# The transfers of the first weight blocks issued ahead of the first keys and queries

## Chip, cores and metric

One Trainium2 chip, one of its cores. The metric is the device time of one execution in microseconds (us), lower is better. The kernel before has a median of 1314.05 us in 3 runs (1313.09 to 1314.7).

## What is computed

Attention with a top-32 mask over 4 batches, 8 heads, 576 tokens, 64 numbers per head, then two gated layers on the 2304 resulting tokens of 512 numbers:

```python
scores = q @ k.T / sqrt(64)                        # 4 x 8 x 576 x 576
scores = where(scores >= 32nd largest of its row, scores, -1e9)
attn = softmax(scores); x = (attn @ v) as 2304 x 512
x = (sigmoid(x @ w_gate) * (x @ w_val)) @ w_out    # 512 -> 1536 -> 512
out = relu(x @ w_in)**2 @ w_out2                   # 512 -> 2048 -> 512
```

q, k and v are float32. The five weights arrive as float64, 34 MB in all.

## The kernel before

The tokens go in chunks: four of 128 (chunks 0 to 3), then seven of 256. Attention works in units, one unit being 128 rows of one head, and 8 units to a chunk of 128. For a unit TensorE makes the scores (`sp`, line 281), ScalarE copies them to SBUF (`S`, 284), VectorE takes the 32 largest of each row by four rounds of MAX8 and three of MATCH_REPLACE8 (`mx`, `W`, 294 and 300), GpSimd and ScalarE mask and exponentiate, TensorE transposes the weights (`tp`) and multiplies with v (`xp`). Keys and queries are first transposed on TensorE (`kpt` 158, `qpt` 244) and split in two parts (`kp`, `kl` 165 and 166; `qt` 256 and 257).

A weight is cut into blocks of 128 x 512, of 512 KB each: 12 of w_gate (`wg`), 12 of w_val (`wv`), 12 of w_out (`wo`), 16 of w_in (`wi`), 16 of the last weight (`w2`, whose tiles print as `w`). `conv` turns two blocks (a pair) to float32: per block ScalarE does two ACTIVATEs (466 and 447), VectorE one TENSOR_SCALAR for the pair (461) and one SCALAR_TENSOR_TENSOR per block (462), GpSimd one integer add per block (467). `scale` then needs products of the converted weight on TensorE (`wg_n`, 484), eight for each pair, and a maximum on VectorE (493). `split` makes two float16 parts of a pair (502 on ScalarE, 505 on VectorE or, for each fourth, 507 and 508 on GpSimd).

Chunk 0 goes through both layers in plain float32 with the converted weights (`moe32`, lines 750 to 833). From chunk 1 on the layers use the split weights in float16: `split_x` scales and splits a chunk's tokens (`x_1cm`, 545, is the maximum of chunk 1 on VectorE), the first layer follows (`pg`, `pv` 593; `acc` 633), its result is scaled in the same way (`x2pq` 666 on TensorE, `x2cm` 668 on VectorE, `x` 672 and 673), then the second layer (`ph` 696, `acc` 717).

Each engine runs its own list in order, SyncE (SP) the list of DMA issues. The order in these lists is made when the kernel is built: every instruction has a priority, which the schedule at the end of the program sets by `at(t)`, and attention heads are drawn forward by `high_priority` (`up[0]`); a planner then places instructions by priority and by its own view of what is ready. `fetch_to(i)` (406) issues the transfers of blocks up to number i, and of up to PREF = 4 blocks behind it while there are tiles left (WSLOTS = 35). Before the change it is called by `conv` alone, so that the first weight transfer has the priority of the first `weight_step`, which lies behind that of the first attention heads.

## Time and profile before

| | us |
|---|---|
| median of 3 runs | 1314.05 |
| profiled execution, span from the first to the last instruction | 1312.3 |
| TensorE busy (span share) | 1214.3 (93%) |
| VectorE busy | 1018.8 (78%) |
| GpSimd busy | 838.6 (64%) |
| ScalarE busy | 758.5 (58%) |

The profiled execution is given by its span alone; the median of the timed runs is 1.75 us above it. Busy shares are averages over stages with different limits, so the table by stage in the section of rows is to be read before them: an engine that is full in a stage sets how long the stage takes, and idle time of the others costs nothing there.

### The profile page before, as it was taken

Reading aid. Unit: us, or ns where it says so; the run is one execution under the profiler, and the core shown is the slowest. Engines: PE = TensorE matmul, PEld = TensorE weight load, DVE = VectorE, ACT = ScalarE, POOL = GpSimd, SP = SyncE. Lnnn points to the kernel's source line nnn. Section 1 sums busy time; section 2 is a strip of 40 time slices with the busy share of each in tenths; the row PEclk is TensorE's granted clock in tenths of the full one; section 3 lists DMA queues with packets and bytes.
Section 4 is the critical chain, followed back from the end, with each engine's and each line's share of the span. In section 5 each row is a group of like instructions: output and inputs, shape, how many; then the busy total and the mean of one; then the engine's idle time right before and its main releaser. Section 6 shows DMA issues by size and latency. Waiting matters only on the chain.

```text
span 1312.3 us, 28283 instructions
## 1 busy us (share of the span) xinstructions
PE 1214.3 (93%) x10613; PEld 971.6 (74%) x10613; DVE 1018.8 (78%) x2192; ACT 758.5 (58%) x1500; POOL 838.6 (64%) x1124
## 2 busy tenths in 40 slices
PE   6746798989999899999999999999999999999998
PEld 4535686777978778777888678777876887787775
DVE  6999999999999999989899888985998698210010
ACT  4876767677666665666566655664566566323122
POOL 1988878888676675586567746674576557324223
PEclk9766899999999999999999999999999999999999
DMA  6967861221323221524211233321111110000000
GB/s 187 350 246 252 276 206 56 62 64 54 94 67 103 61 62 28 132 70 137 82 53 36 73 101 96 95 67 53 42 48 42 46 37 10 17 2 1 17 1 16
DMA packets 116328, 113.00 MB, mean 86 GB/s; under 512 B 73440, under 2 KB 87776, under 8 KB 116192
## 3 DMA queue, kind: packets, MB, share of 16 engines
q1 hardware_dynamic: 116192, 111.19, 28.3%
q8 instruction: 84, 1.38, 0.4%
q14 instruction: 52, 0.43, 0.1%
HBM read 96.99 MB, written 14.16 MB: 85 GB/s over the span
## 4 chain that ended last, share of the span: by engine, by line
PE 70%; DVE 14%; POOL 6%; ACT 3%; DMA 3%; issue 3%; SPq 1%; ACTq 0%; POOLq 0%; DVEq 0%
PE acc L717 13%; PE ph L696 12%; PE pg L593 9%; PE pv L593 9%; PE acc L633 9%; PE xp L373 6%; PE sp L281 6%; PE tp L340 4%; DVE mx L294 3%; DVE W L300 3%; POOL W L307 1%; PE qpt L244 1%; DMA wv_r<-in_moe_w_val_dram 1%; DVE wv_c L462 1%; POOL W L322 1%
## 5 line engine op out<-in xcount | busy, mean ns | idle before, releaser
L294 DVE MAX8 mx<-W 128x8 f32<-128x576 f32 x432 | 327.4, 758 | 7.7
L307 POOL TENSOR_TENSOR W<-S,W 128x576 f32<-128x576 f32 x144 | 208.1, 1445 | 32.6 <-ACT W L306 32.1
L696 PE MATMUL ph<-x,wi_w 128*128 128x256 f16 (+1 forms) x1920 | 209.2, 260 | 8.0 <-ACT x L672 7.4
L300 DVE MATCH_REPLACE8 W<-mx,W 128x576 f32<-128x576 f32 x288 | 213.7, 742 | 0.0
L717 PE MATMUL acc<-w_w,rh 128*128 128x512 f16 x816 | 195.8, 379 | 1.5 <-POOL rh L709 1.5
L696 PEld LDWEIGHTS <-wi_w 128*128 128x128 f16 x1920 | 167.2, 99 | 39.7 <-issue 10.4
L306 ACT ACTIVATE W<-S,bs 128x576 f32<-128x576 f32 x144 | 112.0, 778 | 108.2 <-POOL bs L304 107.9
L593 PE MATMUL pg<-xs,wg_w 128*128 128x256 f16 (+1 forms) x1440 | 156.0, 257 | 3.1 <-ACT xs L547 1.6
L308 ACT ACTIVATE W<-W,bs 128x576 f32<-128x576 f32 x144 | 112.0, 778 | 71.8 <-POOL W L307 71.3
L593 PE MATMUL pv<-xs,wv_w 128*128 128x256 f16 (+1 forms) x1440 | 152.7, 257 | 0.2 <-DVE x2cm L668 0.2
L281 PE MATMUL sp<-kst,qt 128*128 128x288 f32 x608 | 130.6, 327 | 9.0 <-ACT S L284 5.0
L593 PEld LDWEIGHTS <-wg_w 128*128 128x128 f16 x1440 | 122.4, 98 | 18.3 <-issue 2.7
L633 PEld LDWEIGHTS <-wo_w 128*128 128x128 f16 x1440 | 123.1, 98 | 16.6 <-issue 3.7
L593 PEld LDWEIGHTS <-wv_w 128*128 128x128 f16 x1440 | 122.7, 98 | 16.4 <-issue 3.3
L717 PEld LDWEIGHTS <-rh 128*128 128x128 f16 x816 | 77.7, 98 | 76.4 <-POOL rh L709 2.0
L605 DVE TENSOR_TENSOR th<-pv,th 128x512 f32<-128x512 f32 (+1 forms) x60 | 36.2, 603 | 119.1 <-PE pv L593 117.9
L633 PE MATMUL acc<-gh,wo_w 128*128 128x256 f16 (+1 forms) x1200 | 124.8, 254 | 2.4 <-POOL gh L609 2.4
L294 DVE MAX8 mx<-S 128x8 f32<-128x576 f32 x144 | 107.4, 746 | 15.7 <-ACT S L284 15.4
L708 POOL TENSOR_TENSOR r<-r 128x512 f32<-128x512 f32 (+1 forms) x80 | 74.7, 936 | 59.8 <-ACT rh L707 58.8
L341 ACT COPY PT<-tp 128x512 f32<-128x512 f32 x144 | 83.7, 581 | 47.6 <-PE tp L340 39.3
L322 POOL TENSOR_SCALAR we<-W,rz 128x64 f32<-128x64 f32 x128 | 41.5, 324 | 108.0 <-DVE rz L313 72.7
L300 DVE MATCH_REPLACE8 W<-mx,S 128x576 f32<-128x576 f32 x144 | 106.8, 742 | 0.3 <-issue 0.3
(297 smaller groups left out, 2224.8 us busy)
## 6 DMA issues: line engine op xcount, KB each, us to landing
kst<-ks SPq DMA_DIRECT2D x104, 288.0 KB, 2.9
v<-in_v_dram SPq DMA_DIRECT2D x112, 128.0 KB, 2.2
qn<-in_q_dram SPq DMA_DIRECT2D x128, 64.0 KB, 2.2
wi_r<-in_moe_w_in_dram SPq DMA_DIRECT2D x16, 512.0 KB, 6.8
w_r<-in_moe_w_out_dram SPq DMA_DIRECT2D x16, 512.0 KB, 4.7
wg_r<-in_moe_w_gate_dram SPq DMA_DIRECT2D x12, 512.0 KB, 8.0
wv_r<-in_moe_w_val_dram SPq DMA_DIRECT2D x12, 512.0 KB, 7.2
wo_r<-in_moe_w_out_dram SPq DMA_DIRECT2D x12, 512.0 KB, 7.0
```

The source lines that it names most:

```text
L281: nc.tensor.matmul(sp[:, e, 0:HALF], l, r, start=(x == 0), stop=(x == len(ops) - 1))
L294: m8 = nc.vector.max(mx[:, r], cur)
L300: nc.vector.match_replace(wk, mx[:, r], cur, NEG)
L306: nc.scalar.activation(wk, ss, AF.Relu, bias=bs[:, 0:1], scale=-BIG)
L307: nc.gpsimd.tensor_tensor(wk, ss, wk, op=ALU.subtract)
L308: nc.scalar.activation(wk, wk, AF.Exp, bias=bs[:, 1:2], scale=SCALE, accum_out=bs[:, 2:3])
L341: nc.scalar.copy(ptr[:, :, i * P : (i + 1) * P], tp.rearrange("p (c t) -> p c t", c=CB))
L373: nc.tensor.matmul(xp[j * D : (j + 1) * D, o : o + n], vj, pj, start=(si == 0 and c == 0), stop=(c == NB - 1), skip_group_check=True,)
L593: nc.tensor.matmul(pp[:, e * N : (e + 1) * N], wblk(wd, a, c, f0, P), xs[:, b_, c, :], start=(e == 0 and n == 0), stop=(n == 3 * KM - 1), ...
L633: nc.tensor.matmul(acc[:, d // 2, (d % 2) * N : (d % 2 + 1) * N], wblk("wo", a, f, d * P, P), gh[:, b_, e * N : (e + 1) * N], start=(f == ...
L696: nc.tensor.matmul(ph[:, e * N : (e + 1) * N], wblk("wi", a, c, f0, P), x2[:, b_, c, :], start=(e == 0 and n == 0), stop=(n == 3 * KM - 1) ...
L717: nc.tensor.matmul(acc2[:, i, 0:DM], gh[:, b_, e * N + i * P : e * N + (i + 1) * P], wblk("w2", a, f, 0, DM), start=(f == 0 and x == 0), s ...
```

## The change

A constant FIRSTW = 4 is added. Ahead of the schedule's loop stands a new call of `fetch_to` for blocks 0 to 3, at a priority ahead of that of the first attention heads, and the condition in `fetch_to` no longer stops within the first FIRSTW blocks. Comments were taken out too, so line numbers differ by 1 to 6 behind the change.

```diff
+FIRSTW = 4
...
     def fetch_to(i):
         while fetched[0] < len(blocks):
             b = fetched[0]
             spare = b >= len(blocks) - M4RAW
-            if b > i and not (b <= i + PREF and (spare or live[0] + 3 <= WSLOTS)):
+            if b > i and (b >= FIRSTW or i >= FIRSTW) and not (
+                b <= i + PREF and (spare or live[0] + 3 <= WSLOTS)
+            ):
                 break
...
     tw, ta, tm = 0.0, CA0, None
     up[0] = AUP * 50
+
+    at(CA0 - 2 * AUP)
+    fetch_to(FIRSTW - 1)
     body = None
```

`fetch_to(3)` also takes the four blocks that PREF allows behind block 3, so it issues eight. The head of SP's list, before: `kn` and `ke` are keys, `qn` queries, `v` values, `ks` the split keys on their way to DRAM.

```order
L145 DMA kn_0_88<-in_k_dram 128x4x64 x2
L147 DMA ke_0_91<-in_k_dram 64x2x64
L215 DMA qn_0_111<-in_q_dram 128x2x64 x2
L224 DMA v_0_0_114<-in_v_dram 128x256
L227 DMA v_0_0_114<-in_v_dram 64x64
L224 DMA v_0_0_114<-in_v_dram 128x256
L227 DMA v_0_0_114<-in_v_dram 64x64
L172 DMA ks_0_106<-kp_0_93 64x576 x2
```

The same place in the changed kernel:

```order
L423 DMA wg_r_0_88<-in_moe_w_gate_dram 128x1024
L423 DMA wg_r_0_90<-in_moe_w_gate_dram 128x1024
L423 DMA wg_r_0_92<-in_moe_w_gate_dram 128x1024
L423 DMA wg_r_0_94<-in_moe_w_gate_dram 128x1024
L423 DMA wg_r_1_96<-in_moe_w_gate_dram 128x1024
L423 DMA wg_r_1_98<-in_moe_w_gate_dram 128x1024
L423 DMA wg_r_1_100<-in_moe_w_gate_dram 128x1024
L423 DMA wg_r_1_102<-in_moe_w_gate_dram 128x1024
L146 DMA kn_0_104<-in_k_dram 128x4x64 x2
L148 DMA ke_0_107<-in_k_dram 64x2x64
L216 DMA qn_0_127<-in_q_dram 128x2x64 x2
```

Eight weight transfers moved ahead of everything; before, the first of them stood in row 28 of the list. The planner follows them with the work on them. Head of VectorE's list before (keys, queries, then the first unit's maxima):

```order
L166 TENSOR_TENSOR kl_0_94<-kpt_0_0_95,kp_0_93 128x512
L166 TENSOR_TENSOR kl_0_94<-kpt_0_4_102,kp_0_93 128x64
L257 TENSOR_TENSOR qt_0_0_122<-qpt_0_119,qt_0_0_122 128x256
L294 MAX mx_0_185<-S_0_156 128x8
L300 MATCH_REPLACE W_0_184<-mx_0_185,S_0_156 128x576
```

In the changed kernel four pairs are converted first, and this is the end of them and what follows:

```order
L464 TENSOR_SCALAR wg_c_391<-wg_c_391 128x1024
L465 SCALAR_TENSOR_TENSOR wg_c_391<-wg_r_1_100,wg_c_391 128x512
L465 SCALAR_TENSOR_TENSOR wg_c_391<-wg_r_1_102,wg_c_391 128x512
L167 TENSOR_TENSOR kl_0_110<-kpt_0_0_111,kp_0_109 128x512
L167 TENSOR_TENSOR kl_0_110<-kpt_0_4_118,kp_0_109 128x64
L258 TENSOR_TENSOR qt_0_0_138<-qpt_0_135,qt_0_0_138 128x256
L464 TENSOR_SCALAR wg_c_405<-wg_c_405 128x1024
L465 SCALAR_TENSOR_TENSOR wg_c_405<-wg_r_2_314,wg_c_405 128x512
L465 SCALAR_TENSOR_TENSOR wg_c_405<-wg_r_2_316,wg_c_405 128x512
L295 MAX mx_0_201<-S_0_172 128x8
```

The first unit's first maximum moved from row 5 to row 20, behind the conversion of five pairs. On ScalarE's list four more ACTIVATEs 466 come between the steps of pair 2 and those 447 of pair 3; on TensorE's the `wg_n` products of pairs 1 and 2 stand ahead of the first `kpt`, those of pair 3 ahead of the first `qpt`, those of pair 4 among the first `sp`. The third place is VectorE's list where chunk 1's tokens are ready for the layers (`x_1cm`). Before, row 338 and those ahead of it:

```order
L313 RECIPROCAL rz_0_2348<-rz_0_2348 128x1
L505 SCALAR_TENSOR_TENSOR wo_w_1934<-wo_c_978,wos,wo_w_1934 128x1024
L300 MATCH_REPLACE W_1_2404<-mx_1_2405,W_1_2404 128x576
L294 MAX mx_1_2405<-W_1_2404 128x8
L294 MAX mx_2_2481<-S_2_2389 128x8
L300 MATCH_REPLACE W_2_2480<-mx_2_2481,S_2_2389 128x576
L294 MAX mx_2_2481<-W_2_2480 128x8
L545 TENSOR_REDUCE x_1cm<-x_1pq 128x1
```

In the changed kernel, row 349 and those ahead of it:

```order
L301 MATCH_REPLACE W_2_2480<-mx_2_2481,W_2_2480 128x576
L295 MAX mx_2_2481<-W_2_2480 128x8
L508 SCALAR_TENSOR_TENSOR w_w_2185<-w_c_1758,w2s,w_w_2185 128x1024
L301 MATCH_REPLACE W_2_2480<-mx_2_2481,W_2_2480 128x576
L295 MAX mx_2_2481<-W_2_2480 128x8
L508 SCALAR_TENSOR_TENSOR wi_w_2203<-wi_c_1381,wis,wi_w_2203 128x1024
L295 MAX mx_3_2561<-S_3_2444 128x8
L313 TENSOR_SCALAR rz_1_2419<-bs_1_2413 128x1
L548 TENSOR_REDUCE x_1cm<-x_1pq 128x1
```

Counted over the whole list, everything that stood ahead of `x_1cm` still does, and 11 rows more: five splits (two of w_in, two of w_out, one of the last weight), three MAX8, two MATCH_REPLACE8 and a small row. On TensorE's list 14 rows of chunk 0 (four `acc` 814, ten `ph` 797) that stood ahead of the products for `x_1cm` now stand behind them. From the maximum `x2cm` of chunk 2 (row 542 before, 544 after) the lists hold the same rows ahead of each place but for a few neighbours exchanged.

## Rows read from the trace of the kernel before

**Rows 1.** Table by stage: stretch in us, its length, then busy us (and instructions) of TensorE, its weight loads, VectorE, ScalarE, GpSimd, granted TensorE clock, DMA share, GB/s.

```profile
0.00:35.00 35.00, 23.30 (x81) 17.34 (x81) 23.65 (x50) 15.98 (x31) 7.14 (x18) 1.00 0.71 198
35.00:130.00 95.00, 58.08 (x370) 44.68 (x371) 94.78 (x156) 68.61 (x136) 85.32 (x65) 0.68 0.79 281
130.00:250.00 120.00, 99.35 (x806) 83.83 (x806) 114.36 (x208) 82.92 (x151) 100.58 (x91) 0.96 0.50 156
...
330.00:1120.00 790.00, 777.06 (x7017) 623.91 (x7015) 694.31 (x1590) 483.66 (x990) 514.59 (x797) 1.00 0.25 68
```

**Rows 2.** VectorE in order of time, at the maximum that opens chunk 1's layers and at the one that opens chunk 2's second layer; TensorE in order of time, at four products of chunk 0.

```profile
241.84 0.27 DVE L545 TENSOR_REDUCE x_1cm<-x_1pq 128x1 f32<-128x128 f32 x1
...
366.08 0.28 DVE L668 TENSOR_REDUCE x2cm<-x2pq 128x1 f32<-128x128 f32 x1
...
240.00 1.88 PE L814 MATMUL acc<-w_c,rr 128*128 128x512 f32 x4
```

**Rows 3.** Table by stage between these two maxima (columns as in Rows 1).

```profile
241.80:290.00 48.20, 43.27 (x576) 37.65 (x575) 46.65 (x94) 36.28 (x69) 40.39 (x51) 1.00 0.25 70
290.00:310.20 20.20, 16.20 (x174) 13.65 (x174) 19.90 (x42) 14.61 (x29) 16.43 (x19) 0.83 0.19 52
310.20:366.10 55.90, 53.52 (x705) 45.80 (x703) 52.74 (x122) 37.41 (x83) 42.91 (x75) 1.00 0.29 79
```

**Rows 4.** Waits of TensorE from 241.8 to 366.1 us: what waited for what, us in total, times, longest.

```profile
PE ph L696 <- ACT x L672: 3.3, 2, 2.7
PE acc L633 <- POOL gh L609: 1.7, 4, 0.6
PE pg L593 <- ACT xs L547: 1.6, 1, 1.6
PE acc L717 <- POOL rh L709: 1.5, 2, 0.8
PE tp L340 <- POOL W L322: 1.4, 4, 0.6
PE x2pq L666 <- ACT x L664: 0.9, 2, 0.5
PE pg L593 <- POOL xs L557: 0.7, 1, 0.7
```

**Rows 5.** VectorE in order of time (start and duration in us): where it idled in the first 30 us, with idle time and releaser in brackets.

```profile
6.47 0.82 DVE L166 TENSOR_TENSOR kl<-kpt,kp 128x512 fp32r<-128x512 f32 x2 [5.49 <-ACT kp L165]
8.35 0.42 DVE L257 TENSOR_TENSOR qt<-qpt,qt 128x256 fp32r<-128x256 f32 x1 [1.05 <-ACT qt L256]
11.36 0.76 DVE L294 MAX8 mx<-S 128x8 f32<-128x576 f32 x1 [2.59 <-ACT S L284]
...
28.80 0.15 DVE L312 TENSOR_SCALAR rz<-bs 128x1 f32<-128x1 f32 x1 [0.56 <-ACT W L308]
```

**Rows 6.** Transfers, from several views. In order: SP's issue of the first five weight blocks (start, us); ScalarE's wait for the first of them; issue to landing of all `wg_r` blocks; the same of the queries in the first 80 us; from the chain of waits the first keys and the last of the first 14 blocks (start, us); the stretch from 35 to 40 us (columns as in Rows 1).

```profile
25.57 2.51 SPq L420 DMA_DIRECT2D wg_r<-in_moe_w_gate_dram  x5
...
29.82 0.67 ACT L466 ACTIVATE wg_r<-wg_r 128x512 int32<-128x512 uint32 x1 [0.80 <-DMA wg_r<-in_moe_w_gate_dram]
...
DMA to landing us min/median/max: 4.2/8.0/9.7
...
DMA to landing us min/median/max: 1.8/2.3/7.3
...
1.46 3.13 DMA kn<-in_k_dram
...
36.03 9.52 DMA wv_r<-in_moe_w_val_dram
...
35.00:40.00 5.00, 4.21 (x26) 3.73 (x28) 5.00 (x10) 4.95 (x11) 4.21 (x3) 1.00 1.04 413
```

**Rows 7.** The instructions of one line or tile, durations in ns (min/median/max), then first and last start: a split and a conversion step on VectorE. Then ScalarE in order of time, at its pace of one conversion step after another.

```profile
L505 DVE SCALAR_TENSOR_TENSOR wi_w<-wi_c,wis,wi_w x7: 1261/1345/2040, 251.6 to 301.0; 128x1024 f16<-128x1024 f32 x7
...
L462 DVE SCALAR_TENSOR_TENSOR wg_c<-wg_r,wg_c x12: 668/678/1899, 33.1 to 58.5; 128x512 uint32<-128x512 uint32 x12
...
38.42 0.68 ACT L447 ACTIVATE wg_c<-wg_r 128x512 f32<-128x512 f32 x1
38.98 0.69 ACT L466 ACTIVATE wg_r<-wg_r 128x512 int32<-128x512 uint32 x1
```

**Rows 8.** Groups by form in the first 330 us (line, engine, operation, count, busy us, mean ns of one, idle before): conversion and splits on VectorE, conversion on GpSimd.

```profile
L462 DVE SCALAR_TENSOR_TENSOR wg_c<-wg_r,wg_c 128x512 uint32<-128x512 uint32 x12 | 11.3, 973 | 0.0
...
L505 DVE SCALAR_TENSOR_TENSOR wi_w<-wi_c,wis,wi_w 128x1024 f16<-128x1024 f32 x7 | 10.9, 1562 | 0.3 <-ACT wi_w L502 0.3
...
L505 DVE SCALAR_TENSOR_TENSOR wo_w<-wo_c,wos,wo_w 128x1024 f16<-128x1024 f32 x5 | 9.7, 1948 | 2.2 <-ACT wo_w L502 2.2
...
L505 DVE SCALAR_TENSOR_TENSOR w_w<-w_c,w2s,w_w 128x1024 f16<-128x1024 f32 x5 | 7.2, 1436 | 0.5 <-ACT w_w L502 0.5
...
L461 DVE TENSOR_SCALAR wg_c<-wg_c 128x1024 uint32<-128x1024 uint32 x6 | 5.9, 990 | 0.4 <-ACT wg_c L447 0.4
...
L467 POOL TENSOR_TENSOR wg_c<-wg_c,wg_r 128x512 int32<-128x512 int32 x12 | 19.1, 1620 | 1.3 <-ACT wg_c L447 0.7 <-DVE wg_c L462 0.6
```

**Rows 9.** VectorE in order of time: from one MATCH_REPLACE8 of a row block to its next, one MAX8 between.

```profile
25.05 0.74 DVE L300 MATCH_REPLACE8 W<-mx,S 128x576 f32<-128x576 f32 x1
...
26.70 0.74 DVE L300 MATCH_REPLACE8 W<-mx,W 128x576 f32<-128x576 f32 x1
```

## Prediction

> **What bounds the kernel now.** I read first the table by stage, because the busy shares of the whole span (TensorE 93%, VectorE 78%) hide that the limit changes. In the first 35 us no engine is full: VectorE works 23.65 us and idles 11.35. From 35 to 130 us VectorE is full (94.78 of 95), from 130 to 250 nearly so (114.36 of 120), while TensorE has gaps and runs partly at the lower of its two clock levels, 1.2 instead of 2.4 GHz (mean 0.68 of full speed from 35 to 130). From 330 to 1120 us TensorE is full, 777 of 790 [rows 1]. So the kernel has two parts: VectorE's, in which the weights are converted and split and chunks 0 and 1 get their attention, and TensorE's. The time is what TensorE's part takes, plus the time at which it can begin.
>
> Where it begins is read from two places. `x_1cm` at 241.84 us releases chunk 1's tokens for the layers; `x2cm` of chunk 2 stands at 366.08 [rows 2]. Between them TensorE is busy 43.27 + 16.20 + 53.52 = 113.0 of 124.3 us [rows 3]; of its 11.3 us of idle time, 6.5 are waits at the hand-over between layers (3.3 + 1.6 + 0.9 + 0.7) and 4.6 are waits for GpSimd (1.7 + 1.5 + 1.4) [rows 4]. The gaps that the change aims at are VectorE's at the start: 5.49 for the first keys, 1.05 for the queries, 2.59 for the first scores, 0.56 for a sum [rows 5].
>
> **The change part by part.** Nothing is added or removed but order: eight transfers of 512 KB stand ahead of the keys on SP's list, and the planner moves the conversion of these blocks, and more, ahead of attention on every engine.
>
> The keys' transfer. Before, the first keys land at 1.46 + 3.13 = 4.6 us. The first weight block of the run landed 4.2 us after its issue, and ScalarE did wait for it until 29.82. Fourteen blocks issued from 25.57 on had landed at 36.03 + 9.52 = 45.55, so the later ones came each (45.55 - 25.57 - 4.2)/13 = 1.21 us after the one before; 512 KB at the 413 GB/s of the stretch from 35 to 40 us is 1.27. Queries issued behind weights landed after up to 7.3 us, against a median of 2.3: a transfer waits for what was issued ahead of it [rows 6]. With the issues starting at 0.7 us, blocks land from 0.7 + 4.2 = 4.9 us on, 1.25 apart: 6.2, 7.4, 8.7, 9.9, 11.2, 12.4, 13.7. The keys follow at about 15, ten us later than before.
>
> VectorE's start. A pair needs both its blocks converted by ScalarE, 0.56 us a step [rows 7]. Pair 1 can begin on VectorE at 6.9 (6.2 and a step), pair 2 at 9.5. ScalarE's list then has four other steps ahead of pair 3's, the last of them on block 7 (12.4), so that pair begins at about 14.5, pair 4 at its heels. A pair takes VectorE 0.99 + 2 x 0.97 = 2.9 us in the mean, and 0.99 + 2 x 0.67 = 2.3 with its two block steps at their fastest [rows 7, 8]. Pair 1 ends at 9.2 with GpSimd idle, pair 2 at 12.4, pairs 3 and 4 at about 20. GpSimd adds at 1.62 us a block [rows 8], from 8.1 on, and TensorE's list has the products of pairs 1 and 2 ahead of the keys' transposes, those of pairs 3 and 4 ahead of the queries and among the scores. GpSimd is done with pair 2 at about 14.6, so the keys wait for nothing more than their landing; with pair 4 at about 22, which holds the first scores to about 24 and the first MAX8 to 24.6, against 11.36 before. VectorE has the keys, the queries and pair 5 to do in between. Its idle time by then: 6.7 (to 6.9), 0.3, 2.1, 1.0 (queries), 0.7, together 10.8 us. Before it was 11.35 [rows 1]. The hole at the start is filled with weights, but one of nearly the same size opens while weights land. Term: -0.5. Bounds: 6.7 if only the first wait stays (-4.7), and 10.8 plus 1.05 + 2.59 = 3.6, the waits for queries and scores of before [rows 5], if these start afresh when GpSimd is done (+3.1).
>
> Cheaper conversions. Pairs that meet an idle GpSimd cost 2.3 instead of 2.9. Of the four, the first is sure and the third likely: -1.2, between 0 and -2.4 (four times 0.6).
>
> Where chunk 1 comes in VectorE's list. Attention has been pushed behind weights, and the list shows how far it is still behind at `x_1cm`: five splits, three MAX8, two MATCH_REPLACE8 and a small row more stand ahead of it. A MAX8 and a MATCH_REPLACE8 take 1.65 us together [rows 9], so the attention rows take 2 x 1.65 + 0.75 + 0.1 = 4.1. The splits take 5 x 1.26 = 6.3 at their fastest [rows 7] and 2 x 1.56 + 2 x 1.95 + 1.44 = 8.5 at their means [rows 8]. That is 10.4 to 12.6; I take 11, nearer the low end, since rows overlap a little. VectorE is full here, so this is time on the path: `x_1cm` comes at 241.8 - 0.5 - 1.2 + 11 = 251.1.
>
> From there to the second place. The same TensorE work is left, plus 14 rows of chunk 0 that now stand behind chunk 1's first products instead of ahead of them: four 512-wide ones, 1.88 us [rows 2], and ten narrow ones at the stretch's mean, 113.0/1455 = 0.08 each, 0.8; together 2.7. So 115.7 us of work. VectorE is ahead with its splits, so I let the 4.6 us of waits for GpSimd go, and of the 6.5 at hand-overs I let the 14 rows fill the 2.3 at chunk 1's (1.6 + 0.7): 4.2 stay. 251.1 + 115.7 + 4.2 = 371.0, against 366.1: +4.9. With every wait kept (11.3) it is 378.1, +12.0; with none, 366.8, +0.7. VectorE isn't late here: it has 11 us less to do than before in a stretch that it filled for 119.3 us.
>
> Behind `x2cm` of chunk 2 both lists are the same but for neighbours, and TensorE is full [rows 1], so what is lost stays lost. I take +5: a span of 1312.3 + 5 = 1317.3 us. The timed median stands 1.75 above the profiled span, so **1319 us**. A measurement of this kernel can tell about 0.2% (2.6 us) from no change.
>
> **The rivals.** First, **filling the hole pays** (faster). VectorE's idle time is the first thing that one would cure. If the gaps while weights land are smaller than I think, near the 6.7 end, VectorE's part shortens by 4.7 + 1.2 = 5.9; if TensorE can then also catch up what chunk 1 comes later (VectorE has 11 us less to do behind `x_1cm`), the time is 1314 - 6 = 1308. For it: VectorE is full from 35 to 250. Against it: chunk 1's tokens do come later in the list, and TensorE has 113 us to do behind them. The Trainium skill, "Perfetto Trace Analysis", section "Optimization Strategy", says to find the gaps of the engine that limits a regime and make what it waits for start sooner; by that rule the change is right and this rival is the result. What the rows here add is that the gap filled must not be paid for in the start of the next regime.
>
> Second, **it comes out even**. VectorE's sum ahead of `x2cm` is the same set of rows; if TensorE's later start is covered by its 11.3 us of idle time entirely, only VectorE's own terms stay, -0.5 and -1.2, or the +0.7 of the case with no waits at all: 1312 to 1315.
>
> Third, **the keys' delay costs more** (slower still). Before, the chain from the keys over the transposes to the scores waited for nothing but itself; now it stands behind GpSimd's adds and the products of four pairs on TensorE. At its upper bound (+3.1) with no cheaper conversions `x_1cm` comes 14.1 late, and with the sum's own catching up behind it (11.3 of idle time less the 4.2 that stay, less 2.7 of added work: 4.4) 9.7 are left; with half of that catching up, 12: 1326. It decides from the place where GpSimd is later than 22 us with pair 4.
>
> Fourth, the change could do something other than it says: it does, since eight blocks go ahead, not four, but the list shows it, and the sum is made with eight.
>
> **How the numbers follow.** Chances: my forecast, chunk 1 later by some 9 us of which some 5 remain, 0.52; the keys' delay on top, 0.12; even, 0.20; filling pays, 0.16. The forecast's own range is 1315 to 1326 (+0.7 to +12.0). The range that should hold 8 in 10 must reach into the other cases: down to 1309, up to 1327. Slower by over 0.2%: 0.52 + 0.12, less 0.05 for the forecast's low edge, 0.59; within 0.2%: 0.20 + 0.05, of which 0.01 goes to faster, 0.24; faster: 0.17.
>
> **What would show it.** Right: the first `kn` landing near 15 us; VectorE's first MAX8 near 25; VectorE's idle time of the first 35 us near 11; `x_1cm` near 251 and `x2cm` of chunk 2 near 371, and from there on the same distance to the end. Filling pays, if VectorE's idle time is under 8 and `x2cm` comes before 364. The third rival, if the first MAX8 comes behind 28. I am wrong in the step from `x_1cm` on if that comes 10 us later and `x2cm` doesn't: then TensorE had more slack than its waits show.

## The result: 1.2% slower, three times the forecast

The changed kernel takes 1329.99 us, median of 4 runs (1328.17 to 1332.14), against 1314.38 of the kernel before in the same session (4 runs, 1313.09 to 1316.2): ratio 1.0119, 95% interval [1.0099, 1.0139]. That is +15.6 us; +5 was forecast, and the range ended at 1327. The profiled execution has a span of 1327.8 us, 15.5 more than before.

VectorE in order of time (start, duration, idle time in brackets), the first conversions, the queries and the first MAX8; they answer to [rows 5]:

```profile
6.70 0.69 DVE L464 TENSOR_SCALAR wg_c<-wg_c 128x1024 uint32<-128x1024 uint32 x1 [5.71 <-ACT wg_c L450]
7.43 1.29 DVE L465 SCALAR_TENSOR_TENSOR wg_c<-wg_r,wg_c 128x512 uint32<-128x512 uint32 x2
9.28 1.15 DVE L464 TENSOR_SCALAR wg_c<-wg_c 128x1024 uint32<-128x1024 uint32 x1 [0.56 <-ACT wg_c L450]
...
14.22 1.45 DVE L464 TENSOR_SCALAR wg_c<-wg_c 128x1024 uint32<-128x1024 uint32 x1 [1.51 <-ACT wg_c L450]
...
22.77 0.42 DVE L258 TENSOR_TENSOR qt<-qpt,qt 128x256 fp32r<-128x256 f32 x1 [1.05 <-ACT qt L257]
...
26.62 0.76 DVE L295 MAX8 mx<-S 128x8 f32<-128x576 f32 x1 [0.70 <-ACT S L285]
```

So far it is as forecast: pair 1 at 6.7 (6.9), pair 2 at 9.3 (9.5), pair 3 at 14.2 (14.5), the first MAX8 at 26.6 (24.6; 11.36 before). The table by stage (columns as in Rows 1), same stretches as there:

```profile
0.00:35.00 35.00, 14.68 (x76) 10.19 (x76) 23.77 (x32) 21.24 (x37) 20.52 (x20) 1.00 0.91 310
35.00:130.00 95.00, 48.79 (x250) 37.64 (x251) 94.59 (x159) 68.34 (x134) 77.18 (x65) 0.84 0.79 267
130.00:250.00 120.00, 98.85 (x807) 87.37 (x807) 112.84 (x209) 76.53 (x135) 84.69 (x82) 0.86 0.45 131
330.00:1120.00 790.00, 776.60 (x7060) 625.44 (x7057) 687.63 (x1573) 483.13 (x986) 510.30 (x796) 1.00 0.25 68
```

VectorE's column is that of [rows 1] to half a microsecond up to 130 us: one hole was filled, another opened. TensorE's is not: 76 + 250 instructions by 130 us instead of 81 + 370. Now the two places of [rows 2]:

```profile
255.51 0.29 DVE L548 TENSOR_REDUCE x_1cm<-x_1pq 128x1 f32<-128x128 f32 x1
...
310.98 0.29 DVE L671 TENSOR_REDUCE x2cm<-x2pq 128x1 f32<-128x128 f32 x1 [0.23 <-PE x2pq L669]
...
382.79 0.29 DVE L671 TENSOR_REDUCE x2cm<-x2pq 128x1 f32<-128x128 f32 x1 [4.63 <-PE x2pq L669]
```

The row in the middle is `x2cm` of chunk 1, which stood here before:

```profile
289.99 0.29 DVE L668 TENSOR_REDUCE x2cm<-x2pq 128x1 f32<-128x128 f32 x1 [0.30 <-PE x2pq L666]
```

`x_1cm` comes 13.7 us later, `x2cm` of chunk 1 21.0, that of chunk 2 16.7 later, and from there on the distance stays (16.3 at the last `x2cm`, 15.5 at the end). So 7.3 us more are lost in chunk 1's first layer, of which 4.3 come back by chunk 2's `x2cm`. There the whole loss exists. What the engines did until then is read from two stage tables (columns as in Rows 1), first of the kernel before, then of the changed one: up to `x_1cm`, from there to `x2cm`, and both.

```profile
0.00:241.80 241.80, 174.83 (x1206) 141.50 (x1207) 224.59 (x392) 161.09 (x305) 185.09 (x166) 0.85 0.66 216
241.80:366.10 124.30, 113.00 (x1453) 97.11 (x1452) 119.29 (x256) 88.30 (x180) 99.74 (x143) 0.97 0.26 72
0.00:366.10 366.10, 287.82 (x2657) 238.61 (x2658) 343.88 (x647) 249.39 (x484) 284.83 (x308) 0.89 0.52 167
```

```profile
0.00:255.50 255.50, 167.82 (x1171) 139.73 (x1172) 236.29 (x405) 170.29 (x313) 187.01 (x169) 0.87 0.64 204
255.50:382.80 127.30, 118.92 (x1488) 100.90 (x1487) 108.29 (x246) 82.21 (x175) 91.94 (x143) 0.99 0.25 70
0.00:382.80 382.80, 286.74 (x2657) 240.64 (x2658) 344.59 (x649) 252.50 (x487) 278.96 (x312) 0.91 0.51 160
```

The last row of each fence is the account. TensorE has done the same 2657 instructions in both, with 287.8 and 286.7 us of busy time; VectorE has worked 343.9 and 344.6. No work was added: the 16.7 us are idle time, on TensorE 96.1 instead of 78.3, on VectorE 38.2 instead of 22.2. VectorE's lie behind `x_1cm` (127.3 - 108.3 = 19.0 instead of 5.0), TensorE's ahead of it (87.7 instead of 67.0). Behind it TensorE idles a little less than before, 8.4 instead of 11.3, but has more to do. Its waits there answer to [rows 4]:

```profile
PE acc L636 <- POOL gh L612: 5.0, 5, 1.5
PE tp L341 <- POOL W L323: 1.2, 2, 0.9
PE xp L374 <- ACT PT L342: 0.9, 1, 0.9
PE ph L699 <- ACT x L675: 0.8, 1, 0.8
```

And this is the work of chunk 0 that TensorE still has behind `x_1cm` (groups by form: count, busy us, mean ns), before and, in the second fence, after:

```profile
L814 PE MATMUL acc<-w_c,rr 128*128 128x512 f32 x9 | 4.5, 610 | 0.0
L797 PE MATMUL ph<-x_plain,wi_c 128*128 128x128 f32 x12 | 1.5, 275 | 0.0
```

```profile
L817 PE MATMUL acc<-w_c,rr 128*128 128x512 f32 x20 | 9.3, 596 | 0.0
L800 PE MATMUL ph<-x_plain,wi_c 128*128 128x128 f32 x32 | 4.4, 275 | 0.0
```

13.7 us of chunk 0 stand behind `x_1cm` instead of 6.0.

### The profile page after: what moved, and what is told of

The parts are those of the page before. It is cut to its first block, busy times and chain, and to the rows that moved or that the text cites. A ratio compares the mean times of both kernels' runs of the same rounds, so it can differ in the third digit from the quotient of the medians.

```text
span 1327.8 us, 28308 instructions
## 1 busy us (share of the span) xinstructions
PE 1213.1 (91%) x10613; PEld 974.7 (73%) x10613; DVE 1021.1 (77%) x2192; ACT 762.8 (57%) x1500; POOL 829.7 (62%) x1124
## 4 chain that ended last, share of the span: by engine, by line
PE 75%; DVE 11%; POOL 4%; ACT 4%; DMA 3%; issue 2%; SPq 1%; ACTq 0%; POOLq 0%; DVEq 0%
PE acc L720 13%; PE ph L699 13%; PE acc L636 9%; PE pv L596 9%; PE pg L596 9%; PE xp L374 7%; PE sp L282 6%; PE tp L341 4%; DVE mx L295 3%; DVE W L301 2%; POOL W L308 1%; PE qpt L245 1%; DVE wi_c L465 1%; PE pg L753 1%; DMA w_r<-in_moe_w_out_dram 1%
## 5 line engine op out<-in xcount | busy, mean ns | idle before, releaser
L282 PE MATMUL sp<-kst,qt 128*128 128x288 f32 x608 | 133.3, 331 | 20.5 <-ACT S L285 12.7
L596 PEld LDWEIGHTS <-wv_w 128*128 128x128 f16 x1440 | 122.2, 98 | 15.2 <-issue 1.8
L282 PEld LDWEIGHTS sp<-kst,qt 128*128 128x128 f32 x608 | 91.3, 192 | 32.7 <-ACT S L285 14.4
```

The lines of the kernel that those rows point to most:

```text
L282: nc.tensor.matmul(sp[:, e, 0:HALF], l, r, start=(x == 0), stop=(x == len(ops) - 1))
L596: nc.tensor.matmul(pp[:, e * N : (e + 1) * N], wblk(wd, a, c, f0, P), xs[:, b_, c, :], start=(e == 0 and n == 0), stop=(n == 3 * KM - 1), ...
```

## The experiments

Each run has the kernel before beside it; differences below are against its median in the same session. This table holds what is compared. "Unit 8" is when VectorE ended the last MAX8 of chunk 0's attention, in brackets how many of the 34 pairs its list converts ahead of that; then the two places of above, and the number of instructions that TensorE had done by 241.8 us, read from stage tables.

| kernel | us against before | first MAX8 | unit 8 (pairs) | x_1cm | x2cm, chunk 2 | TensorE by 241.8 |
|---|---|---|---|---|---|---|
| before | 0 | 11.4 | 105.0 (16) | 241.8 | 366.1 | 1206 |
| changed | +15.6 | 26.6 | 130.9 (25) | 255.5 | 382.8 | 1058 |
| e1 four blocks | +18.0 | 17.7 | 137.2 (25) | 256.6 | 383.3 | 1040 |
| e2 behind the first unit | +15.9 | 11.3 | 113.6 (20) | 254.4 | 380.2 | 1109 |
| e3 splits held | +18.9 | 26.4 | 130.7 (25) | 252.6 | 384.5 | 1079 |
| e4 late keys alone | +22.3 | 27.6 | 127.7 (21) | 263.7 | 387.3 | 1003 |
| e5 early, held | +25.9 | 11.2 | 122.2 (16) | 260.3 | 392.0 | 1069 |
| e6 changed, held | +37.2 | 23.9 | 129.7 (16) | 267.3 | 397.9 | 1043 |
| e7 other order | +10.6 | 11.1 | 108.2 (17) | 245.6 | 377.7 | 1139 |
| e8 attention first, early | +34.8 | 11.2 | 110.0 (12) | 271.5 | 397.9 | 1062 |
| x1 emission only | +9.2 | 11.2 | 104.7 (16) | 241.0 | 376.1 | 1201 |
| x2 late layer | +9.9 | 11.0 | 104.7 (16) | 239.5 | 375.4 | 1174 |
| x3 attention first | +16.4 | 11.0 | 91.8 (12) | 253.9 | 381.7 | 1166 |
| x4 early, held whole | +18.3 | 11.1 | 113.8 (16) | 259.1 | 384.9 | 1111 |
| y1 spacing | 0.0 | 11.1 | 104.6 (16) | 236.8 | 366.4 | 1229 |
| y2 late shift | +1.5 | 11.2 | 104.6 (16) | 239.0 | 367.7 | 1222 |
| y3 early, near order | +19.3 | 11.3 | 116.9 (16) | 258.8 | 389.5 | 1134 |
| y4 behind two pairs of heads | +10.4 | 11.4 | 111.0 (18) | 246.7 | 378.6 | 1136 |
| z1 as y4, held | +14.8 | 11.2 | 116.3 (16) | 249.5 | 386.5 | 1148 |
| z2 four blocks, as z1 | +7.8 | 11.3 | 108.6 (16) | 243.9 | 372.0 | 1197 |

**e1, exactly four blocks.**

```diff
-    def fetch_to(i):
+    def fetch_to(i, pref=PREF):
...
-                b <= i + PREF and (spare or live[0] + 3 <= WSLOTS)
+                b <= i + pref and (spare or live[0] + 3 <= WSLOTS)
...
-    fetch_to(FIRSTW - 1)
+    fetch_to(FIRSTW - 1, 0)
```

> As the changed kernel, but exactly four blocks go ahead of the first keys (nothing behind them), so VectorE's list begins with the keys, the queries and the first MAX8 as before the change. VectorE's list at x_1cm is still that of the changed kernel: the same five splits, three MAX8 and two MATCH_REPLACE8 more stand ahead of it than before. Theory A, the place in the list (the loss is the rows that VectorE does ahead of x_1cm): x_1cm near 253, time near 1328. Theory B, the late start (the loss is what TensorE and VectorE don't get done while attention waits; 15.3 us at the first MAX8 have become 15.6 at the end, about one for one): the first MAX8 near 16.5, 5 us later than before, time near 1319.

1330.87 against 1312.85, ratio 1.0138 [1.0121, 1.0155]. The first MAX8 came 9 us earlier than in the changed kernel and nothing was won: theory B's 1319 is off by 12, theory A's 1328 by 3. Halving the blocks doesn't halve the loss.

**e2, eight blocks behind the first unit's keys.**

```diff
                 if n == 0:
-                    keys(0)
-                    pr.load()
-                    pr.load_keys(0)
-                    pr.queries(pr.tts[0:1])
+                    with tc.high_priority(offset=int(3 * AUP * 50)):
+                        keys(0)
+                        pr.load()
+                        pr.load_keys(0)
+                        pr.queries(pr.tts[0:1])
```

> All eight blocks ahead, but behind the keys, queries and values of the first unit, which are issued as before. VectorE's list at x_1cm (row 350) has the same five splits and five attention rows more ahead of it as in the changed kernel. Theory A: x_1cm near 253, time near 1328. Theory B: the first MAX8 at 11 to 12 as before, nothing lost at the start, 1312 to 1316; below 1312 if blocks that land some 15 us earlier then fill VectorE's first gaps.

1328.76, ratio 1.0122 [1.0107, 1.0137]. The first MAX8 stands where it stood before (11.26 us), and the loss is the whole +15.9. Theory B falls: it isn't the late first unit. Theory A's 1328 fits so far. But later units still come late: the second pair of heads' keys, now behind the blocks, land at 23.5 us instead of 12.7, and unit 3 ends at 51.1 instead of 30.7.

**e3, the extra splits held behind x_1cm.**

```diff
+    h0 = [t[1:] for t in todo].index(("wo", 3))
+    held, todo = todo[h0:], todo[:h0]
...
+    while 1 not in xsp:
+        attend(emitted[0] + 1, AHEAD)
+    p0 = tc.cur_priority
+    at(tm - SUP)
+    hold[0] = True
+    for t in held:
+        split(*t[1:])
+    tc.cur_priority = p0
```

(With `hold`, the ACTIVATE and the VectorE instruction of a split are ordered behind `x_1cm`.)

> As the changed kernel, but the splits from w_out's fourth on are held behind x_1cm by an order of the list without a wait on a semaphore: none of the five extra splits stands ahead of x_1cm. Theory A: x_1cm comes 5 x 1.4 = 7 us earlier, near 248.5, and the time falls to about 1323. Theory B: the splits were done in time that TensorE could not use anyway, x_1cm may come earlier but x2cm of chunk 2 stays near 383 and the time at 1328 to 1331.

1331.74, ratio 1.0144 [1.0128, 1.0159]. `x_1cm` comes 2.9 us earlier than in the changed kernel instead of 7, `x2cm` of chunk 2 1.7 later. Theory A falls too: the splits have to be done anyway, and the end doesn't care on which side of `x_1cm`.

**e4, late keys without early blocks** (the kernel before plus eight dummy transfers to DRAM).

```diff
     up[0] = AUP * 50
+    at(CA0 - 2 * AUP)
+    for kt in range(8):
+        t = dpool.tile([P, 1024], U32, tag=f"dm{kt}", name=f"dm_{kt}")
+        nc.sync.dma_start(t, w_out2[kt * P : (kt + 1) * P, 0:512].bitcast(U32))
```

> The kernel before, with eight transfers of 512 KB of the last weight into a scratch place in DRAM ahead of the first keys: the keys come late as in the changed kernel, but no weight block comes early and nothing is converted in the meantime; the output is the same. If the early conversions of the changed kernel are worth what they cost VectorE (four pairs at about 2.5 us, 10 us), this is about 10 us slower than the changed kernel, 1338 to 1342. Theory B (what counts is when attention begins, the early conversions return little): the first MAX8 near 22 to 26 and 1324 to 1331. Theory A: the same five splits stand ahead of x_1cm here, so 1328 plus the time that VectorE stands at the start, 1335 or more.

1335.10, ratio 1.0174 [1.0159, 1.0189]. With the keys late and no weight block early, 22.3 us are lost. That is 6.6 us above the changed kernel's +15.6. In the first 35 us VectorE works 10.66 instead of 23.77:

```profile
0.00:35.00 35.00, 9.48 (x39) 6.80 (x39) 10.66 (x19) 11.08 (x19) 7.12 (x11) 1.00 0.88 282
```

So the early conversions are worth something, some 7 us for 13 that VectorE worked more, but only where the change itself has made the hole. Theory A's "1335 or more" is met, but the planner exchanged rows here too (21 pairs ahead of unit 8 instead of 16), so not all of the 22.3 need be the keys'.

**e5 and e6, conversions held to their old place among the units.** NEED[p] is the number of units that stood ahead of pair p before the change; e5 has it on e2, e6 on the changed kernel.

```diff
+            maxima.append(m8.ins)
...
+                        i0 = nc.vector.tensor_scalar(ci, ci, 3, None, op0=ALU.logical_shift_left)
+                        if NEED[nstep[0]]:
+                            tc.add_manual_dep(
+                                i0.ins, maxima[min(NEED[nstep[0]], len(maxima)) - 1].name, NOSYNC, reason="behind a unit"
+                            )
...
-            elif tw <= ta and nstep[0] < len(steps):
+            elif tw <= ta and nstep[0] < len(steps) and emitted[0] >= NEED[nstep[0]]:
```

> Transfers as in the run with eight blocks behind the first unit's keys (1328.8), but each pair's conversion on VectorE is held behind the last MAX8 of the unit that it followed before the change: 16 pairs converted ahead of the last MAX8 of unit 8 (the end of chunk 0's attention) instead of 20, as before. Only VectorE's order is held, no wait is added. Theory C (early blocks are converted in place of attention; chunk 0's attention ends later, TensorE gets its layer-one products later and has the work to do when it is full): time 1311 to 1316, chunk 0's first product at 97 to 102. Theory D (the early transfers themselves cost, by what they take from keys and queries in the queue and on the DMA engines): 1326 or more, as without the hold.

> The changed kernel with the same hold: eight blocks ahead of the first keys, conversions behind the units that they followed before the change. Theory C: the loss from displaced attention goes, only the late start stays. Keys at 15 us instead of 4.6, VectorE stands still in between, the first MAX8 near 21: 8 to 10 us late, chunk 0's first product near 109, time 1322 to 1325. If the late start costs nothing by itself: 1312 to 1316. Theory D: 1330 or more.

1339.16, ratio 1.0196 [1.0174, 1.0219], and 1350.44, ratio 1.0282 [1.0252, 1.0312]. Both are far above what theory C allowed, and where theory D (the early transfers cost by themselves) put them. The waits of e5's TensorE in the first 60 us show one reason:

```profile
PE kpt L160 <- DMA kn<-in_k_dram: 16.4, 3, 9.7
```

It was 5.2 us in two waits before. The second pair of heads' keys are now behind the blocks, unit 3 ends at 35.9 instead of 30.7, and since the hold keeps conversions out of the hole, VectorE stands still. The second reason is in the last section. Theory C isn't tested cleanly by these two, but conversions kept out of attention's way didn't cure the loss.

**e7, another order without early blocks** (the kernel before).

```diff
-        head(0)
+        with tc.high_priority(offset=int(3 * AUP * 50)):
+            head(0)
```

> The kernel before with a higher priority for all that belongs to the start of attention (the second pair of heads' keys and queries too): no weight goes ahead of anything, but the planner's order shifts a little everywhere: 17 pairs instead of 16 ahead of unit 8's last MAX8, x_1cm at row 339 instead of 338. Theory C: one pair more is 3 us at chunk 0's first product, time 1314 to 1318. Theory E (the order before was a lucky one, and whatever shifts it costs some 15 us): near 1328.

1323.85, ratio 1.0080 [1.0058, 1.0102]: above theory C's 1314 to 1318, below theory E's 1328.

**e8 and x3, attention further ahead**: 12 pairs ahead of unit 8, in e8 on e5's transfers, in x3 on the kernel before, there held from ScalarE's two steps on (the diff shows the first).

```diff
-                nc.scalar.activation(c[:, e], r.bitcast(F32)[:, :, 1], AF.Copy, scale=REBIAS)
+                i0 = nc.scalar.activation(c[:, e], r.bitcast(F32)[:, :, 1], AF.Copy, scale=REBIAS)
+                if NEED[nstep[0]]:
+                    tc.add_manual_dep(i0.ins, maxima[min(NEED[nstep[0]], len(maxima)) - 1].name, NOSYNC, reason="behind a unit")
```

> Transfers as in e5, but held further: 12 pairs instead of 16 ahead of unit 8's last MAX8 (w_gate and w_val whole, which chunk 0's first layer needs), the others later. Theory C carried on: chunk 0's first product 8 to 12 us earlier, near 90, and as much of it as TensorE's wait for w_out's pairs doesn't take back: 1304 to 1311. If VectorE's total by x_1cm is the limit and not chunk 0's start: 1312 to 1320.

> The kernel before, with conversions held behind units from ScalarE's first step on (not only on VectorE as in e8): 12 pairs instead of 16 ahead of unit 8. Transfers as before the change. Theory C: unit 8 ends 8 to 10 us earlier, chunk 0's first product near 90, time 1306 to 1314. Theory F (conversions that are held meet GpSimd and cost VectorE 1.24 us a block step in place of 0.88, as in e5 and e8): unit 8 not before 105, time 1325 or more.

1348.04, ratio 1.0276 [1.0243, 1.0309], and 1329.64, ratio 1.0132 [1.0114, 1.0149]. x3 moves no transfer: unit 8 ends at 91.8, 13 us early, and the kernel is 16.4 us slower; chunk 0's first product stays at 99.2. Theory F fits in time only, since it wanted unit 8 behind 105. Attention further ahead doesn't pay either.

**x1 and x2, chunk 0's layers ordered behind a unit** (LATE = 8, where they stand anyway, and 10; no transfer or conversion is moved).

```diff
-            if body is None and ci in xsp:
+            if body is None and ci in xsp and emitted[0] >= LATE:
...
+                        if fp == 0 and t == e == c == 0:
+                            tc.add_manual_dep(mm.ins, maxima[LATE - 1].name, NOSYNC, reason="behind a later unit")
```

> The kernel before, with chunk 0's first product ordered behind the last MAX8 of unit 8, where it stands anyway: nothing moves on purpose, VectorE's list has the same pairs ahead of each unit (16 ahead of unit 8), TensorE's list the same row for the first product. The planner still exchanges neighbours. Theory C (what counts is when chunk 0's attention ends and its layers can begin): first product near 100, time 1313 to 1317. Theory E (any exchange costs some 10 us, the order before is a lucky one): 1322 to 1328, as with the other order (1323.9).

> As x1, but chunk 0's first product is ordered behind the last MAX8 of unit 10: no transfer and no conversion is moved, VectorE still has 16 pairs ahead of unit 8, only TensorE begins chunk 0's layers some 27 to 32 us later, as in the changed kernel (128.9 against 99.8). Theory C: TensorE's work that can't be done early has to be done when it is full: 1323 to 1330, and 8 us or more above x1. If TensorE makes up for it, because it waits for w_val and w_out in the kernel before anyway: within 3 us of x1.

1322.44, ratio 1.0070 [1.0052, 1.0088], and 1323.14, ratio 1.0075 [1.0058, 1.0091]. In x2 the first product starts at 141.3 us, later than in the changed kernel (129.0), and it costs 0.7 us over x1: theory C falls, the late start of chunk 0's layers is no price by itself. But x1, which should have done nothing, lost 9.2, as theory E had it. Its stage up to `x2cm` of chunk 2:

```profile
0.00:376.10 376.10, 297.46 (x2657) 247.47 (x2658) 342.49 (x649) 253.20 (x487) 288.22 (x312) 0.86 0.51 162
```

The same 2657 instructions, idle 78.6 us as before (78.3), but 297.5 us busy instead of 287.8: x1 loses its 10 us in how long TensorE's instructions take, at a mean granted clock of 0.86 of full speed instead of 0.89. The changed kernel loses idle time at 0.91. They are different losses.

The other runs can be read in the same way, since TensorE has done 2657 instructions at this place in each of them. Against the kernel before, e7, x1, x2 and x3, which have no transfers ahead, show 0.3 to 5.8 us more idle time and 5.8 to 11.6 more busy time. z2 and y4 show 5.4 and 6.5 more idle time, all other runs with transfers ahead, e4's dummies among them, 10.7 to 27.9. In one profiled execution of each, idle time of TensorE is the mark of the transfers, slower instructions that of a shifted order.

**x4 and y3, early blocks held from ScalarE's steps on** (e2's transfers; x4 holds both ACTIVATEs of a block, y3 the first).

> As e5 (eight blocks early behind the first unit's keys, 16 pairs ahead of unit 8), but held from ScalarE's steps on, so that ScalarE's second step of a block doesn't run ahead and GpSimd's adds come when they came before the change. Theory F: VectorE's block step falls from 1.24 to about 0.9 us, 20 us less in all; unit 8 ends near 108 to 112 (second pair of heads' keys still 5 us late), time 1314 to 1322. If the early transfers themselves are the cost: 1330 or more as in e5.

> Eight blocks early behind the first unit's keys, conversions held on ScalarE's first step so that the lists come as near to those of before as they get: 16 pairs ahead of unit 8, x_1cm at row 337, 100 products of chunk 1's second layer ahead of chunk 2's maximum, and x2cm of chunk 2 and 3 at the rows of before (542, 680). Theory H: second pair of heads' keys 5 us late, 1316 to 1321. Theory G: 1322 to 1332. If the early transfers are a cost by themselves, near 1331 to 1339 as in x4 and e5.

1331.49, ratio 1.0139 [1.0120, 1.0157], and 1333.30, ratio 1.0143 [1.0117, 1.0170]. VectorE's block steps cost 0.96 and 1.02 us in the mean instead of e5's 1.24, so theory F names a true part of e5 (x4 is 7.6 us below it), but not 20 us. The rest stays, with unit 3 again 7 us late (37.8 and 38.0). Both are in the ranges that their texts gave for early transfers as a cost by themselves (1330 or more, 1331 to 1339).

**y1 and y2, small shifts of the kernel before** (CA = 6.1 instead of 6.0; SWI = 4 instead of 5).

> The kernel before with one number of the schedule changed by 2% (the distance of attention's priorities, 6.0 to 6.1). Transfers, the start and VectorE's list are the same up to row 188; behind it neighbours are exchanged (x_1cm stays at row 338, 104 products of chunk 1's second layer ahead of chunk 2's maximum on TensorE's list instead of 109). Theory G (the order of before is one that the planner's rules rarely find; whatever shifts it costs 8 to 11 us from x_1cm to x2cm of chunk 2): 1320 to 1326. Theory H (what counts there is how much of chunk 1's second layer TensorE has ahead of chunk 2's maximum: 109 before, 8 after the change, 72, 48 and 34 in three controls): 1313 to 1316.

> The kernel before with the last conversions of w_in asked for one step of chunk 0's layers earlier: the lists are the same up to VectorE's row 252, and 113 products of chunk 1's second layer stand ahead of chunk 2's maximum. Theory G: 1319 to 1326. Theory H: 1312 to 1316.

1313.98, ratio 0.9997 [0.9986, 1.0009], and 1315.51, ratio 1.0007 [0.9993, 1.0021]. Theory G, that any shift costs, falls, and theory E with it.

**y4, z1 and z2, blocks behind two pairs of heads** (e7's edit on the changed kernel; z1 with y3's hold; z2 with e1's edit too).

> Eight blocks ahead, but behind the keys, queries and values of the first two pairs of heads (units 1 to 4): 18 pairs instead of 16 ahead of unit 8, x_1cm at row 339 as before, and 8 products of chunk 1's second layer ahead of chunk 2's maximum as in the changed kernel. Theory H: x_1cm near 245, time 1324 to 1330. Theory G: 1320 to 1328 too. If what costs is VectorE's list at the start (pairs ahead of unit 8: 16 before, 20 to 25 in the early kernels), about 2 pairs x 2.5 = 5 us: 1317 to 1320.

> Transfers as in y4 (eight blocks behind the keys, queries and values of the first two pairs of heads), but conversions held on ScalarE's first step, so that 16 pairs instead of 18 stand ahead of unit 8's last MAX8, and 92 products of chunk 1's second layer ahead of chunk 2's maximum instead of 8. Theory I (the blocks don't cost by themselves; they cost where VectorE converts them in place of attention, or where later heads' keys come late behind them): unit 8 ends near 106 as before, time 1314 to 1319, 5 us or more below y4 (1324.4). If the hold itself costs what it saves, as in x4 and y3 against e2: 1324 to 1332.

> As z1, but four blocks, exactly; the lists come nearest to those of before of all kernels with early blocks (16 pairs ahead of unit 8, x_1cm at row 338, x2cm at rows 413, 542 and 680 as before). Theory I: 1313 to 1317. If early blocks cost whatever their place: above 1322.

1324.38, ratio 1.0074 [1.0055, 1.0093]; 1331.15, ratio 1.0117 [1.0092, 1.0141]; 1324.12, ratio 1.0074 [1.0046, 1.0101]. Theory H fits y1, y2 and y4, but not y3, of which it wanted 1316 to 1321. y4 has the same edit as e7, on the changed kernel instead of the kernel before, so e7 is its control: +10.4 and +10.6 us, `x2cm` of chunk 2 at 378.6 and 377.7. y4's blocks are issued from 14.56 us on, e7's from 20.21. Behind the keys of two pairs of heads the earlier blocks cost nothing that shows beyond the shift of order.

Theory I fails as a forecast: with 16 pairs ahead of unit 8 z1 is slower than y4 with 18. Its units 1 to 3 end as before (30.7), unit 4 at 52.1 instead of 44.4: TensorE waits 5.9 us for the third pair of heads' keys, and VectorE converts three pairs between unit 4's first MAX8 and its next step. In time z1 and z2 are where their texts had them if the blocks or the hold cost anyway (1324 to 1332, above 1322). z2, with half the blocks, is level with y4 in ratio; these two are the best of the kernels with early blocks, and slower than before. No run beat the kernel before.

## Why the forecast was right in sign and wrong in size

**The start was right**, the keys (landed at 14.3 and 14.9 us, forecast 15), the order of the pairs, the first MAX8 to 2 us, the idle time: 35 - 23.77 = 11.2 us in the first 35 against 11.35, forecast 10.8. A hole of the same size opened while blocks land. (The transfer issued at 36.03 us is the thirteenth block, not the fourteenth, so the pace worked out from it is 1.32 us, not 1.21; the sum took 1.25, and the eight blocks landed 1.29 apart.)

**"Cheaper conversions" had the wrong sign.** -1.2 was taken; they cost 3.8 us more. The 68 block steps on VectorE went from 59.9 to 64.8 us, the 34 pair steps from 38.1 to 37.0. The first and the third pair were cheap, as forecast (1.29 us for two block steps each), the later ones dearer, most of all the last weight's and w_in's:

```profile
L465 DVE SCALAR_TENSOR_TENSOR w_c<-w_r,w_c 128x512 uint32<-128x512 uint32 x16 | 17.1, 1105 | 0.0
L465 DVE SCALAR_TENSOR_TENSOR wi_c<-wi_r,wi_c 128x512 uint32<-128x512 uint32 x16 | 16.6, 1075 | 0.0
```

(890 and 826 ns before.) The step priced the four pairs that are moved, not the thirty whose surroundings change with them. What changed there is how long the block steps wait for GpSimd (last section).

**"Where chunk 1 comes in VectorE's list" was right in its rows.** 11 was taken; the splits came to +4.0 us (26.4 instead of 22.4) and the attention rows to +4.3, 8.3 in all. With 3.8 for conversions, 2.0 more idle time, and what small rows and overlaps take off, that is the 13.7 at `x_1cm`, where 9.3 had been forecast.

**"From there to the second place" is the step that failed most.** It let TensorE catch up 4.4 us, to 115.7 of work and 4.2 of waits; measured are 118.9 and 8.4, 3.0 us more than before instead of 4.4 less. These 7.4 us, and 4.4 by which `x_1cm` came later than forecast (255.5 instead of 251.1), are the 11.8 between 371.0 and 382.8. Two terms are off. The 2.7 us of chunk 0's work behind `x_1cm`, counted from rows of the list, were 7.7: the list tells the order, not how far TensorE has got when VectorE reaches a row. (The rest of the work took 1.8 us less than before, at a granted clock of 0.99.) And the 4.6 of waits for GpSimd, let go because VectorE would be ahead with its splits, became 6.2 (5.0 + 1.2). "VectorE isn't late here" was true and no use: it idles 19.0 us there.

**What replaced it.** Attention came later, and with it TensorE's work. The second pair of heads' keys landed at 29.4 us instead of 12.7, and up to 130 us VectorE was as full as before, but on weights: 25 pairs ahead of unit 8 instead of 16. TensorE had done 447 instructions at 160 us instead of 599, and 1058 instead of 1206 at 241.8. Behind that TensorE is nearly full and gets little of it back. The last column of the table shows this across kernels: 1197 to 1229 go with losses of 0 to 9 us, 1109 to 1174 with 10 to 19, 1079 and fewer with 15.6 to 37. That is a regularity over 20 kernels; no run varied it alone. Among the rivals, "the keys' delay costs more" came nearest in time (1326). Its mark, a first MAX8 behind 28, wasn't reached, and e2 loses as much with the first unit on time. But its subject was the right one: late keys without early blocks lose 22.3 us in e4. It priced the first keys and left out the later ones, which stand behind the blocks in e2 too.

**The rule** of the Trainium skill, "Perfetto Trace Analysis", section "Optimization Strategy", says to make what the limiting engine waits for start sooner. Here its gain shows, some 7 us between e4 and the changed kernel, and is less than the 22.3 us that e4 loses without it.

**What stays open.** How the 15.6 us divide between the late keys, the conversions in attention's place, and the order that the planner happens to find. As far as e4 tells, late keys are enough for such a loss, and with conversions held to their old place it remains (e5, e6, x4, y3), so theory D, that the transfers cost by what they take from keys and queries, survives for blocks that stand ahead of the second pair of heads' keys: the nine such kernels, the changed one among them, lose 15.6 to 37. Behind those keys it isn't shown: y4 and z2 lose no more than the shift e7, z1 loses 14.8. And the shifts e7, x1 and x2 lose 9 to 11 where y1 and y2 lose next to nothing; why is open, but in x1 and x2 it is mostly busy time. A kernel with the early transfers and every other list untouched wasn't tried.

## What to carry to other kernels

When transfers move ahead, ask what then stands behind them, not only for the first keys but for the next ones, and what the scheduler will do with the data that come early. Here VectorE was as busy as before and TensorE starved, and TensorE pays later, when it is full; so count each engine's finished instructions at the point where it becomes the limit. Idle time at the start is only worth filling with what doesn't push back the work that feeds the engine that limits later. And where a planner sets the order, run a control that shifts the order and nothing else: some here cost as much as two thirds of the change, others nothing.

## What the runs showed of the hardware that was not expected

VectorE's slow block steps are those that wait for GpSimd's running instruction to end. In e5, VectorE and, in the second fence, GpSimd in order of time; the last row of each is one instruction by itself:

```profile
86.27 8.06 DVE L472 SCALAR_TENSOR_TENSOR wv_c<-wv_r,wv_c 128x512 uint32<-128x512 uint32 x6
L472 DVE SCALAR_TENSOR_TENSOR wv_c<-wv_r,wv_c x6: 678/1766/1778, 86.3 to 92.6; 128x512 uint32<-128x512 uint32 x6
87.47 1.78 DVE L472 SCALAR_TENSOR_TENSOR wv_c<-wv_r,wv_c 128x512 uint32<-128x512 uint32 x1
```

```profile
87.03 8.44 POOL L477 TENSOR_TENSOR wv_c<-wv_c,wv_r 128x512 int32<-128x512 int32 x5 [0.62 <-DVE wv_c L472]
87.03 1.67 POOL L477 TENSOR_TENSOR wv_c<-wv_c,wv_r 128x512 int32<-128x512 int32 x1 [0.62 <-DVE wv_c L472]
```

The six steps (shortest, median, longest in ns) are of two kinds, 0.68 us and 1.77. The one that starts at 87.47, in the middle of an add, ends at 89.25, 0.55 us behind the add's end at 88.70. It is so for every slow step: of the 68 block steps 30 take over 0.72 us in the kernel before, 25 in the changed one and 43 in e5, and each of them ends 0.53 to 0.58 us behind the end of a GpSimd instruction. What they take above 0.68 each sums to 16.1, 21.2 and 41.2 us. That is where the dearer conversions of the changed kernel come from, and e5's: over its 68 steps the busy time was 1.24 us a step against 0.88 before, 24 us more, of which its 34 pair steps gave 13 back (0.74 instead of 1.12).

The Trainium skill, "SBUF — State Buffer", section "Who interferes with whom", says that a VectorE instruction with two SBUF inputs contends with a GpSimd instruction that reads SBUF, and calls contention for the port pair that the two share an exclusive lock. The trace agrees: the step above waits for the add's end and takes 1.1 us longer than the shortest.

TensorE's granted clock was 1.00 (2.4 GHz throughout) from 40 to 80 us in the changed kernel and 0.66 in the mean (partly 1.2 GHz) in the kernel before, though TensorE did fewer instructions in the changed one (99 against 158) and was busy about as long. From 105 to 160 us it is the other way round, 0.59 with TensorE busy 26.6 of 55 us against 0.78 with 36.2. In the first fence the changed kernel, in the second the one before:

```profile
40.00:80.00 40.00, 24.11 (x99) 18.35 (x97) 39.66 (x76) 29.96 (x61) 29.19 (x26) 1.00 0.95 313
105.00:160.00 55.00, 26.64 (x165) 21.66 (x166) 54.93 (x91) 33.38 (x66) 47.10 (x40) 0.59 0.63 196
```

```profile
40.00:80.00 40.00, 25.58 (x158) 19.06 (x154) 40.00 (x69) 29.44 (x59) 36.01 (x29) 0.66 0.94 336
105.00:160.00 55.00, 36.24 (x264) 30.78 (x262) 53.55 (x101) 39.13 (x78) 47.51 (x42) 0.78 0.85 289
```
